# Attention then a gated MLP on one core: MLP work begins with step 21 instead of step 12, and the weights' conversion is spread anew

## The chip, the cores and the metric

The kernel runs on one core of one Trainium2 chip. The metric is the device time of one execution in microseconds (us); a figure for a kernel is the median of several runs. One execution was also taken by the hardware profiler, and all rows of a profile below come from such an execution.

## The reference, cut to what matters

Random-feature attention over 8 batches of 8 heads, 576 rows and 64 columns with 128 features, and a gated MLP on its 4608 output rows (model width 512, inner width 1536). Everything is in 32-bit floats.

```python
def phi(x):
    proj = np.einsum('bhsd,md->bhsm', x, omega)
    sq = np.sum(x * x, axis=-1, keepdims=True) / 2.0
    h = proj - sq
    h = h - np.max(h, axis=-1, keepdims=True)
    return np.exp(h) / np.sqrt(m)
q_p, k_p = (phi(q_s), phi(k_s))
kv = np.einsum('bhsm,bhsd->bhmd', k_p, v)
z = np.sum(k_p, axis=2)
num = np.einsum('bhsm,bhmd->bhsd', q_p, kv)
den = np.einsum('bhsm,bhm->bhs', q_p, z)[..., None] + 1e-06
attn_out = num / den
x = attn_out.transpose(0, 2, 1, 3).reshape(B * S, H * D)
g = x @ w_gate
out = (g * (1.0 / (1.0 + np.exp(-g))) * (x @ w_val)) @ w_out
```

The MLP's three weights arrive as 64-bit floats and are converted by the kernel, word by word, to 32-bit floats.

## The kernel before, in words

**Attention** runs in 72 steps. A step takes two groups of 256 rows of q or k: first twelve groups of k, then a group of q with a group of k in each step. Nine groups make a batch, one of the nine being the odd rest of all heads (its loads are four smaller transfers). The list `ORDER` (L671) sets what a step issues: project x on the features (`st_project`, L377, 16 matrix multiplications in two PSUM banks `pp`), put q's result of three steps ago in transposed form into the MLP's input (`q_out`, L520), transpose the next step's rows (`st_transpose`, L358, bank `pt`; GpSimd squares the rows, L372), multiply q's features with the k-v sums (`q_mult`, L486, bank `po`), accumulate k-v sums (`k_accumulate`, L440), maxima and squares' sums on VectorE (`st_max`, L394), transpose q's features (`q_transpose`, L473, bank `ptq`), and exponentials on ScalarE (`st_exp`, L412, eight of them). The instructions are then put in an order of each engine by the framework; each engine runs its own list in order.

**The MLP** works on ten column tiles of x (256 columns, eight times 512, 256) and on four sets of three inner blocks; one tile with one set is a visit. A visit has 72 multiplications of `mm1` (L550, lines L558; gate `g`, then value `v`) and 9 of `mm2` (L561, L567, output `o`) per 128 rows of the tile. It is written as a generator, `stream` (L600), and yields after every bundle; `give` (L657) draws from it what the plan has due. A product of 32-bit floats is made of three multiplications with high and low parts, which ScalarE (L237, L543, L641) and GpSimd or VectorE (L238, L642, L544) split.

**The conversion** (`convert_all`, L242) takes 36 pieces, three weights for each of twelve inner blocks. A piece has seven ticks: one ScalarE operation (L255), five on VectorE (L257 to L265) and one on GpSimd (L267), of 512 elements in each of 128 partitions; the last also stores the piece to a scratch in memory (L270, on SyncE's queue) and, for the first nine pieces, splits it for the MLP's first set. Every piece loads its raw words first (L220, L225). `need` (L281) forces ticks when the MLP asks for a piece that isn't converted.

**The plan** is made of tables before any instruction is issued. `whole[j]` is the step from which tile j's input is complete (12 for tile 0, 21 for tile 1, 30 for tile 2), `upper` the MLP work that can be done by a step, `lower` what must be, and `course` a smooth line between them: the MLP work to be given by each step. `marks` pairs steps with numbers of pieces that are to be converted by then; in between, ticks follow the plan's clock. `EARLY` (L200) is the step up to which projections of odd steps and the transposed features of q take banks of the MLP's pool (four banks `ps_m`); afterwards projections share two banks and the rest of attention one bank (`ps_a`). `DENSE` (L201) is the same for the transposes of x.

**Queues.** All transfers are issued by SyncE in one list: loads of q, k (`nat`, three buffers, asked for three steps ahead), v, raw weights, stores of converted pieces, loads of weights for later sets, and the output.

Of the kernel before, what the change touches and what calls it, by code (L numbers as in the profile page):

```python
# [23 lines left out]
def kernel(  # L24
# [25 lines left out]
    FA = 3  # L50
# [111 lines left out]
    def visit_us(j):  # L162
        w = TILES[j][1]
        return 2 * FA * mm1_us(w) + w // P * MM2

    cum = np.concatenate([[0.0], np.cumsum([visit_us(j) for j, _, _ in visits])])

    whole, begun = {}, {}
# [5 lines left out]
                begun.setdefault(j, n + OLAG)  # L174


    NN = NS + OLAG + 1
    upper, lower = np.zeros(NN + 1), np.zeros(NN + 1)
    for n in range(NN + 1):
        vi = 0  # L180
        while vi < len(visits) and whole[visits[vi][0]] < n:
            vi += 1
        upper[n] = cum[vi]
        lower[n] = max([0.0] + [cum[last_visit[j - NXB] + 1] for j in begun if j >= NXB and begun[j] <= n])
    lower = np.minimum(lower, upper)
    course = (lower + upper) / 2
    course[0], course[NN] = 0.0, upper[NN]
    for _ in range(20000):
# [3 lines left out]
        course[2:-1:2] = np.clip(mid[1::2], lower[2:-1:2], upper[2:-1:2])  # L192


    clock = course + 4.0 * np.arange(NN + 1)
    marks = [(0, 0.0), (whole[0] - 1, FA), (whole[0] + 2, 3 * FA)]
    for k_ in range(1, NSET):
        at = int(np.searchsorted(course, cum[len(ROUNDS[0]) * k_ - 1]))
        marks.append((max(at, marks[-1][0] + 1), 3 * FA * (k_ + 1)))
    EARLY = whole[0]  # L200
    DENSE = marks[2][0] + 20  # L201

# [130 lines left out]
    def load(n):  # L335
        if n >= NS:
            return
        nats[n] = att.tile([P, 2, CH, 2, D], F32, name=f"nat{n}", tag="nat", bufs=3)
        for kind, src in (("q", q), ("k", k)):
            for i, b, _, gr in slots(n, kind):  # L340
                load_group(nats[n][:, i], src, b, gr, False)
# [16 lines left out]
    def st_transpose(n):  # L358
        if n >= NS:
            return  # L360
        nat = nats.pop(n)
        pt = (ps_moe if n < DENSE else ps_att)(f"pt_{n}", [P, 2, G])
        for i in range(2):
            for c in range(CH):
                nc.tensor.transpose(  # L365
                    pt[:, i, c * P : (c + 1) * P], nat[:, i, c].rearrange("p h d -> p (h d)"), ident
                )
        x = att.tile([P, 2, G], F32, name=f"x_{n}", tag="x")

        st = att.tile([P, 4, 2, CH, 2], F32, name=f"st_{n}", tag="st", bufs=6)  # L370
        sq = att.tile([P, 2, CH, 2, D], F32, name=f"sq_{n}", tag="sq")
        nc.gpsimd.tensor_tensor(sq, nat, nat, op=ALU.mult)  # L372
        nc.scalar.copy(x, pt)
        sts[n] = x, st, sq
        return True

    def st_project(n):  # L377
# [3 lines left out]

        new = ps_moe if n < EARLY and n % 2 else ps_proj
        pp = [new(f"pp{hh}_{n}", [P, 2, CH, M]) for hh in range(2)]
# [89 lines left out]
    def q_transpose(n):  # L473
        m = n
        n -= TLAG
        for _, b, g, gr in slots(n, "q"):
            ph = box.pop(("q", b, g))
            pt = (ps_moe if m < EARLY else ps_att)(f"ptq{b}_{g}", [P, 2, G])
            for hh in range(2):
# [210 lines left out]
    st_transpose(0)  # L690
    for n in range(NN):
        load(n + LA)
# [42 lines left out]
```

## Time and profile before

| | |
|---|---|
| median of three runs | 1291.54 us (1289.42 to 1296.39) |
| profiled execution, its own time | 1285.57 us |
| its span in the profile | 1283.8 us |
| granted TensorE clock, mean | 0.982 |
| idle TensorE in the first 31.6 us | 10.8 us |
| idle TensorE from 31.6 to 217.3 us | 14.0 us |
| idle TensorE from 217.3 us to the end | 15.7 us |

The profile lists the engines' busy time, the chain of work that ended last, groups of equal instructions by line with the mean duration of one, and the busy time of each engine in chosen stretches. TensorE's multiplications are pipelined, so a busy TensorE can still be waiting for its input or running slower than it could. A step is told from the next by the first of its 16 projections (L388): step 4 begins at 31.6 us, step 9 at 50.1, step 12 at 64.0, step 13 at 71.7, step 17 at 121.3, step 20 at 140.0, step 21 at 152.4, step 30 at 217.3 and step 35 at 383.6 us.

### The profile page before, as it was taken

To read this page: it belongs to the slowest core of one execution; us is meant where nothing else is said; L and a number is where in the kernel's file an instruction comes from. 1 tells how busy PE (TensorE), PEld (TensorE's weight loads), DVE (VectorE), ACT (ScalarE), POOL (GpSimd) and SP (SyncE) were. 2 spreads that over 40 slices of the span, in tenths; PEclk is the share of its full clock that TensorE was granted. 3 is DMA by queue.
4 is the path that set the end of the run, shared out by engine and by line. 5 is a ranking of instruction groups with operands and counts; after the bars stand their busy time and mean duration, and the time that the engine had idled before them with its cause. 6 is when DMAs were issued, how large, how long until landed. Compare 5 with 4: busy or idle time off the path is not lost.

```text
span 1283.8 us, 19309 instructions
## 1 busy us (share of the span) xinstructions
PE 1243.3 (97%) x7329; PEld 1039.1 (81%) x7329; DVE 514.2 (40%) x1080; ACT 629.0 (49%) x1358; POOL 419.1 (33%) x364
## 2 busy tenths in 40 slices
PE   6988999999989999999999999999999999999998
PEld 5977778887868888888878888888888878888887
DVE  4787774457742343223333333223333321121212
ACT  4865666565344554555556653854544323222211
POOL 3454241545444121333333311433322113242421
PEclk7997899999989999999999999999999999999999
DMA  6557552345432122221222221211110111111112
GB/s 161 137 159 192 141 160 63 86 136 154 125 95 62 42 67 63 60 64 50 65 59 50 65 51 41 66 50 50 51 41 26 34 33 34 41 43 32 50 27 57
DMA packets 156477, 95.71 MB, mean 75 GB/s; under 512 B 119520, under 2 KB 131808, under 8 KB 156384
## 3 DMA queue, kind: packets, MB, share of 16 engines
q1 hardware_dynamic: 156384, 94.47, 28.0%
q8 instruction: 58, 0.95, 0.3%
q14 instruction: 35, 0.29, 0.1%
HBM read 75.56 MB, written 18.87 MB: 74 GB/s over the span
## 4 chain that ended last, share of the span: by engine, by line
PE 81%; DVE 7%; ACT 3%; issue 3%; POOL 2%; DMA 2%; SPq 1%; POOLq 0%; ACTq 0%; DVEq 0%
PE o L567 21%; PE g L558 21%; PE v L558 19%; PE pp L388 6%; PE kvacc L458 5%; PE po L497 4%; PE ptq L481 2%; PE pt L365 2%; ACT ph L420 1%; PE xt L527 1%; DVE st L261 1%; DVE st L406 1%; POOL wlo L238 1%; DMA nat<-in_k_dram 1%; SPq L323 1%
## 5 line engine op out<-in xcount | busy, mean ns | idle before, releaser
L642 POOL TENSOR_TENSOR hl<-sl,hh 128x512 fp32r<-128x512 f32 (+1 forms) x120 | 145.0, 1208 | 288.9 <-ACT hh L641 285.6
L238 POOL TENSOR_TENSOR wlo<-wraw,whi 128x512 fp32r<-128x512 f32 x108 | 138.9, 1299 | 251.7 <-ACT whi L237 230.0
L420 ACT ACTIVATE ph<-pp,st 128x128 f32<-128x128 f32 x576 | 166.6, 388 | 55.1 <-DVE st L409 54.0
L558 PE MATMUL g<-xh,whi 128*128 128x512 f32 (+1 forms) x480 | 184.4, 387 | 0.5 <-DVE sl L638 0.4
L558 PE MATMUL v<-xh,whi 128*128 128x512 f32 (+1 forms) x480 | 184.0, 383 | 0.0
L567 PE MATMUL o<-whi,hh 128*128 128x512 f32 x432 | 178.1, 412 | 2.4 <-ACT whi L237 1.7
L558 PE MATMUL g<-xl,whi 128*128 128x512 f32 (+1 forms) x480 | 180.0, 375 | 0.0
L558 PE MATMUL g<-xh,wlo 128*128 128x512 f32 (+1 forms) x480 | 178.8, 372 | 0.0
L558 PE MATMUL v<-xh,wlo 128*128 128x512 f32 (+1 forms) x480 | 178.1, 371 | 0.0
L558 PE MATMUL v<-xl,whi 128*128 128x512 f32 (+1 forms) x480 | 177.6, 370 | 0.0
L567 PE MATMUL o<-wlo,hh 128*128 128x512 f32 x432 | 171.5, 397 | 2.0 <-DVE st L408 1.4
L567 PE MATMUL o<-whi,hl 128*128 128x512 f32 x432 | 171.2, 396 | 0.3 <-POOL hl L642 0.2
L641 ACT CAST hh<-sl 128x512 fp32r<-128x512 f32 (+1 forms) x120 | 69.9, 584 | 172.7 <-DVE sl L638 172.3
L638 DVE TENSOR_TENSOR sl<-v,sl 128x512 f32<-128x512 f32 (+1 forms) x120 | 76.3, 636 | 188.0 <-PE v L558 181.9
L372 POOL TENSOR_TENSOR sq<-nat 128x512 f32<-128x512 f32 x72 | 77.4, 1076 | 213.0 <-DMA nat<-in_k_dram 192.8
L591 DVE TENSOR_TENSOR acc<-o,acc 128x512 f32<-128x512 f32 x108 | 74.3, 690 | 178.4 <-PE o L567 177.9
L406 DVE TENSOR_REDUCE st<-pp 128x4 f32<-128x512 f32 x144 | 93.5, 684 | 103.0 <-PE pp L388 103.0
L237 ACT CAST whi<-wraw 128x512 fp32r<-128x512 f32 x108 | 66.9, 623 | 103.9 <-PE v L558 58.5
L558 PEld LDWEIGHTS g<-xh,wlo 128*128 128x128 f32 x480 | 91.3, 190 | 15.2
L558 PEld LDWEIGHTS g<-xh,whi 128*128 128x128 f32 x480 | 91.2, 191 | 15.3 <-DVE sl L638 0.6
L558 PEld LDWEIGHTS v<-xh,wlo 128*128 128x128 f32 x480 | 90.4, 188 | 15.3
L558 PEld LDWEIGHTS g<-xl,whi 128*128 128x128 f32 x480 | 91.6, 191 | 13.2 <-DVE xl L544 0.3
(56 smaller groups left out, 1872.1 us busy)
## 6 DMA issues: line engine op xcount, KB each, us to landing
wraw<-wscr SPq DMA_DIRECT2D x108, 256.0 KB, 2.8
wscr<-wc SPq DMA_DIRECT2D x36, 256.0 KB, 2.2
out_dram<-acc SPq DMA_DIRECT2D x72, 128.0 KB, 2.3
nat<-in_k_dram SPq DMA_DIRECT2D x64, 128.0 KB, 3.1
v<-in_v_dram SPq DMA_DIRECT2D x64, 128.0 KB, 3.1
nat<-in_q_dram SPq DMA_DIRECT2D x64, 128.0 KB, 2.7
st<-in_moe_w_gate_dram SPq DMA_DIRECT2D x12, 512.0 KB, 4.4
st<-in_moe_w_val_dram SPq DMA_DIRECT2D x12, 512.0 KB, 4.6
```

Source lines behind the costliest of these rows:

```text
L237: nc.scalar.copy(hi, raw)
L238: nc.gpsimd.tensor_tensor(lo, raw, hi.bitcast(F32), op=ALU.subtract)
L372: nc.gpsimd.tensor_tensor(sq, nat, nat, op=ALU.mult)
L388: nc.tensor.matmul(pp[hh][:, i, c, :], x[r, i, c * P : (c + 1) * P], omT[r], start=True, stop=True)
L406: nc.vector.tensor_reduce(st[:, 1, :, :, hh], pp[hh], axis=AX.X, op=ALU.max, negate=True)
L420: nc.scalar.activation(ph[:, c, hh * M : (hh + 1) * M], pp[hh][:, i, c, :], AF.Exp, bias=st[:, 3, i, c, hh : hh + 1], scale=1.0,)
L558: nc.tensor.matmul(ps, a_[:, ws], b_[:, c, :], start=n == 0, stop=n == 3 * NC - 1)
L567: nc.tensor.matmul(ps, a_[:, ts_], b_, start=first and n == 0, stop=last and n == 2)
L591: nc.vector.tensor_tensor(a_, po, a_, op=ALU.add)
L638: nc.vector.tensor_tensor(h, pv, h, op=ALU.mult)
L641: nc.scalar.copy(hh, h)
L642: nc.gpsimd.tensor_tensor(hl, h, hh.bitcast(F32), op=ALU.subtract)
```

## The change

`upper` is held at zero through step 21, so the MLP's first visits, of tile 0 and tile 1 with the first set, are planned together in steps 21 to 29. The plan's MLP work per step was 1.4 us in steps 12 to 20 and 2.7 us in steps 21 to 29 (its own units); it is now 0 and 4.1 us. From step 30 on the course is the same. `EARLY` is 21 instead of 12. The marks of the conversion were three pieces by step 11, nine by step 14, and then 18, 27 and 36 by steps 30, 33 and 35; now six by step 21, nine by step 23, and the same three. `DENSE` was 34 and is 35.

```diff
-        upper[n] = cum[vi]
+        upper[n] = cum[vi] if n > whole[1] else 0.0
...
+    EARLY = whole[1]
     clock = course + 4.0 * np.arange(NN + 1)
-    marks = [(0, 0.0), (whole[0] - 1, FA), (whole[0] + 2, 3 * FA)]
+    marks = [(0, 0.0), (EARLY, 2 * FA), (EARLY + 2, 3 * FA)]
     for k_ in range(1, NSET):
         at = int(np.searchsorted(course, cum[len(ROUNDS[0]) * k_ - 1]))
         marks.append((max(at, marks[-1][0] + 1), 3 * FA * (k_ + 1)))
-    EARLY = whole[0]
-    DENSE = marks[2][0] + 20
+    DENSE = marks[-1][0]
```

Lines of the changed kernel are one higher than before from L184 on. In the rows below, `pp0_13` is a projection of step 13, `st_13` its maxima and sums, `v0_1` the MLP's value of visit 0 and block 1, `wc1_1` the piece of block 1 and weight 1 (0 gate, 1 value, 2 output).

TensorE before, in step 13, within the first visit:

```order
L558 MATMUL g0_2_1119<-xh0_657,wlo2_0_533 128x256
L365 MATMUL pt_15_1142<-ident_87,nat15_877 128x128 x4
L458 MATMUL kvacc2_0_1164<-v0_94,ph1_12_980 128x65 x4
L558 MATMUL v0_0_1214<-xh0_657,whi0_1_803 128x256
L558 MATMUL v0_0_1214<-xl0_658,whi0_1_803 128x256
L497 MATMUL po0_5_1047<-kvr0_0_383,qt0_5_969 128x65 x4
L558 MATMUL v0_0_1214<-xh0_657,wlo0_1_804 128x256
```

TensorE of the change, at the same place, step 13:

```order
L389 MATMUL pp1_13_935<-omT_93,x_13_886 128x128
L366 MATMUL pt_14_956<-ident_87,nat14_790 128x128 x4
L482 MATMUL ptq0_6_983<-ident_87,ph0_12_917 128x128 x4
L459 MATMUL kvacc2_0_1050<-v0_94,ph1_12_922 128x65 x2
L528 MATMUL xt0_4_945<-ident_87,xn0_4_899 128x128 x2
L389 MATMUL pp0_14_1008<-omT_93,x_14_961 128x128
```

The MLP's rows are gone from steps 12 to 19; the first of them now stand in step 20 (20 of `g`), and all others of both visits in steps 21 to 29.

VectorE before, behind the last operation of `st_max` of step 12:

```order
L409 SCALAR_TENSOR_TENSOR st_12_821<-st_12_821 128x8
L257 TENSOR_SCALAR wc1_1_847<-wc1_1_847 128x512
L504 TENSOR_SCALAR dn0_4_938<-po0_4_933 128x4
L259 TENSOR_SCALAR wc1_1_847<-wc1_1_847 128x512
L505 RECIPROCAL dn0_4_938<-dn0_4_938 128x4
L261 SCALAR_TENSOR_TENSOR st1_1_801<-st1_1_801,wc1_1_847 128x512
L507 TENSOR_TENSOR xn0_4_941<-po0_4_933,dn0_4_938 128x256
L263 TENSOR_SCALAR wc1_1_847<-st1_1_801 128x512
L257 TENSOR_SCALAR wc2_1_918<-wc2_1_918 128x512
L265 SCALAR_TENSOR_TENSOR wc1_1_847<-st1_1_801,wc1_1_847 128x512
L259 TENSOR_SCALAR wc2_1_918<-wc2_1_918 128x512
L261 SCALAR_TENSOR_TENSOR st2_1_843<-st2_1_843,wc2_1_918 128x512
```

VectorE of the change, behind the same operation:

```order
L410 SCALAR_TENSOR_TENSOR st_12_820<-st_12_820 128x8
L400 TENSOR_REDUCE st_14_962<-sq_14_963 128x8
L264 TENSOR_SCALAR wc1_1_1022<-st1_1_738 128x512
L505 TENSOR_SCALAR dn0_4_896<-po0_4_891 128x4
L266 SCALAR_TENSOR_TENSOR wc1_1_1022<-st1_1_738,wc1_1_1022 128x512
L506 RECIPROCAL dn0_4_896<-dn0_4_896 128x4
L407 TENSOR_REDUCE st_13_887<-pp0_13_934 128x4
L508 TENSOR_TENSOR xn0_4_899<-po0_4_891,dn0_4_896 128x256
L407 TENSOR_REDUCE st_13_887<-pp1_13_935 128x4
```

Ten operations of conversion stood ahead of step 13's maxima; two stand there now. Before, eight pieces are worked on by VectorE in steps 12 to 16 and some five in steps 21 to 29; in the change some three in steps 12 to 20, and twelve in steps 21 to 29.

VectorE of the change, behind the maxima of step 22:

```order
L258 TENSOR_SCALAR wc2_2_1706<-wc2_2_1706 128x512
L545 TENSOR_TENSOR xl2_1314<-xt1_4_1683,xh2_1313 128x256
L260 TENSOR_SCALAR wc2_2_1706<-wc2_2_1706 128x512
L410 SCALAR_TENSOR_TENSOR st_22_1564<-st_22_1564 128x8
L262 SCALAR_TENSOR_TENSOR st2_2_1604<-st2_2_1604,wc2_2_1706 128x512
L505 TENSOR_SCALAR dn1_5_1713<-po1_5_1708 128x4
L264 TENSOR_SCALAR wc2_2_1706<-st2_2_1604 128x512
L506 RECIPROCAL dn1_5_1713<-dn1_5_1713 128x4
L639 TENSOR_TENSOR sl0_2_1666<-v0_2_1758,sl0_2_1666 128x256
```

Between the maxima of steps 22 and 23 ten operations of conversion now stand, where two stood before; some of them, and the MLP's products, stand between the two halves of `st_max`. From step 31 on the lists of VectorE and TensorE have the same instructions in each step as before. ScalarE gets six more loads of its function table (102 in all, 96 before), since its silu and exponentials alternate more often.

## The prediction

> **What bounds the kernel now.** I read the page first, its busy times and the slices.
>
> ```profile
> span 1283.8 us, 19309 instructions
> PE 1243.3 (97%) x7329; PEld 1039.1 (81%) x7329; DVE 514.2 (40%) x1080; ACT 629.0 (49%) x1358; POOL 419.1 (33%) x364
> ...
> PEclk7997899999989999999999999999999999999999
> ...
> PE 81%; DVE 7%; ACT 3%; issue 3%; POOL 2%; DMA 2%; SPq 1%; POOLq 0%; ACTq 0%; DVEq 0%
> ```
>
> TensorE (PE) bounds the kernel as a whole: it is busy for 97% and carries 81% of the chain that ended last. But the early slices have a granted clock below 9 tenths, and the chain has 7% of VectorE (DVE). So I cut the span at the beginnings of the steps in question, taken from the first projection (L388) of steps 12, 21 and 30 in the timeline, and asked for the engines' busy times between them (columns: stretch, its length, busy time of PE, weight loads, DVE, ACT, POOL with instructions, granted clock, DMA share, GB/s).
>
> ```profile
> 64.03 0.49 PE L388 MATMUL pp<-omT,x 64*128 64x128 f32 x4
> ...
> 152.36 0.49 PE L388 MATMUL pp<-omT,x 64*128 64x128 f32 x4
> ...
> 217.29 0.49 PE L388 MATMUL pp<-omT,x 64*128 64x128 f32 x2
> ```
>
> ```profile
> 31.60:50.10 18.50, 18.41 (x189) 16.79 (x188) 14.79 (x36) 15.59 (x51) 7.61 (x7) 1.00 0.65 157
> 50.10:64.00 13.90, 13.55 (x132) 12.44 (x132) 11.04 (x29) 11.76 (x37) 6.19 (x7) 1.00 0.47 111
> 64.00:71.70 7.70, 7.55 (x70) 7.11 (x69) 6.25 (x16) 5.77 (x20) 3.23 (x3) 1.00 0.84 242
> 71.70:121.30 49.60, 40.94 (x269) 34.60 (x268) 42.00 (x81) 27.40 (x69) 28.30 (x23) 0.83 0.61 168
> 121.30:152.40 31.10, 28.51 (x192) 24.72 (x191) 22.83 (x56) 17.70 (x54) 8.74 (x8) 0.89 0.63 162
> 152.40:217.30 64.90, 62.71 (x472) 53.02 (x471) 44.04 (x111) 43.00 (x120) 18.56 (x15) 1.00 0.44 118
> 217.30:383.60 166.30, 158.17 (x872) 132.44 (x871) 94.64 (x161) 85.05 (x156) 76.03 (x60) 0.98 0.39 115
> 383.60:1283.80 900.20, 892.65 (x5019) 739.92 (x5018) 263.83 (x566) 409.66 (x822) 258.49 (x216) 1.00 0.19 49
> ```
>
> The rows are steps 4 to 8, 9 to 11, 12, 13 to 16, 17 to 20, 21 to 29, 30 to 34 and the rest. Steps 9 to 11, the whole of attention without MLP, take 13.9 / 3 = 4.63 us each. Steps 13 to 16 take 49.6 / 4 = 12.4 us each: there VectorE is busy for 42.0 of 49.6 us, TensorE idles for 8.7 us, and its clock is granted at 0.83. That is the one stage which another engine bounds. From 217.3 us on the work is TensorE's again, with 15.7 us of idle time in 1066.
>
> The waits from 64 to 152 us and, for SyncE's queue, from 60 to 217 us show how the stage is tied (columns: who waited for whom, us in total, times, longest):
>
> ```profile
> POOL wc L267 <- DVE wc L265: 24.3, 8, 6.8
> ...
> SPq L270 <- POOL wc L267: 40.3, 15, 4.7
> ```
>
> GpSimd waits for VectorE's conversion, and SyncE's list, behind whose store of a piece (L270) the loads of q and k are queued, waits for GpSimd.
>
> **The MLP work that is moved.** The chain in order of time has runs of multiplications without a gap (start, us, what, count):
>
> ```profile
> 66.98 1.19 PE g L558 x10
> ...
> 582.46 2.82 PE g L558 x12
> ...
> 599.10 2.14 PE o L567 x9
> ```
>
> One of 256 columns takes 1.19 / 10 = 0.119 us, one of 512 takes 2.82 / 12 = 0.235, one of the output 2.14 / 9 = 0.238. The first visit, of 256 columns, is 72 x 0.119 + 18 x 0.238 = 12.9 us. Twenty of its multiplications (2.4 us) now stand in step 20, the other 10.5 us behind step 21. Steps 21 to 29 of before hold 62 of 512 columns and 36 of the output, 14.6 + 8.6 = 23.1 us, so attention costs TensorE (64.9 - 23.1) / 9 = 4.64 us a step beside MLP work, the same as 4.63 without it.
>
> **Steps 12 to 20** took 152.4 - 64.0 = 88.4 us. With the MLP's work and the burst of conversion gone (some three pieces are left on VectorE), they are like steps 9 to 11, which have the same banks, the same loads and a similar rate of conversion: 9 x 4.63 + 2.4 = 44.1 us. The banks matter here: with the old bound of 12 the projections of every step share two banks, and steps 17 to 19, with little MLP work, show what that gives at most:
>
> ```profile
> 121.30:140.00 18.70, 17.84 (x137) 15.75 (x136) 14.63 (x39) 12.93 (x41) 4.55 (x5) 1.00 0.57 143
> ```
>
> That is 6.2 us a step, MLP included; the upper bound is 9 x 6.2 = 56 us. The lower one is the mean of steps 4 to 11, (18.5 + 13.9) / 8 = 4.05, or 38.9 us with the 2.4. I take 44.1, since steps 9 to 11 are the only ones with all of attention and no burst. Hidden here is VectorE, ACT and the transfers: DVE was 11.0 of 13.9 us and ACT 11.8, so neither has much to spare; if one becomes the bound, the bound of 56 us covers it. The loads of q, k and v go with the steps, and the stretch of steps 4 to 8 moved 157 GB/s at 3.7 us a step.
>
> **Steps 21 to 29** get the MLP work and seven pieces. TensorE's need is 9 x 4.64 + 52 x 0.119 + 72 x 0.235 + 54 x 0.238 = 41.8 + 36.0 = 77.8 us, the lower bound. VectorE's need starts from the 44.0 us that it has there now. The first rows are those of 152.4 to 217.3 us, the last two those of 71.7 to 121.3 us (mean ns behind the bar):
>
> ```profile
> L261 DVE SCALAR_TENSOR_TENSOR st<-st,wc 128x512 int32<-128x512 int32 x5 | 4.4, 886 | 0.2
> L265 DVE SCALAR_TENSOR_TENSOR wc<-st,wc 128x512 f32<-128x512 uint32 x5 | 3.5, 690 | 0.0
> L259 DVE TENSOR_SCALAR wc<-wc 128x512 int32<-128x512 int32 x5 | 3.1, 623 | 0.1
> L263 DVE TENSOR_SCALAR wc<-st 128x512 int32<-128x512 int32 x5 | 2.1, 420 | 0.0
> L257 DVE TENSOR_SCALAR wc<-wc 128x512 f32<-128x512 f32 x5 | 2.1, 414 | 0.7 <-ACT wc L255 0.7
> ...
> L261 DVE SCALAR_TENSOR_TENSOR st<-st,wc 128x512 int32<-128x512 int32 x8 | 8.6, 1077 | 0.1
> L263 DVE TENSOR_SCALAR wc<-st 128x512 int32<-128x512 int32 x8 | 5.5, 687 | 0.1
> ```
>
> A piece is 0.886 + 0.690 + 0.623 + 0.420 + 0.414 = 3.03 us of VectorE. Seven more make 21.2; two sums of squares at about 0.68 and three products of 256 columns at about 0.42 (estimates from the sizes of these rows) make 2.7. That is 68 us. Where conversion was dense, L261 took 1.077 and L263 0.687 us, 0.46 us more a piece, so twelve pieces may cost 5.5 us more: 68 to 73.5 us. In steps 13 to 16 the stretch was 49.6 / 42.0 = 1.18 times VectorE's busy time; that factor gives 80 to 87 us, and as VectorE will be about as dense here, this row is nearer than TensorE's bare need. I take 84 us. ScalarE gets some of its six added table loads here, at the duration of the first row below, and 7 x 0.704 us of L255, the second; its 43.0 us grow to about 60 of 84, so it is covered. Should nothing cover the table loads, each stops the exponentials behind it, 6 x 1.3 = 7.7 us, so the upper bound is 87 + 7.7 = 95 us.
>
> ```profile
> L420 ACT ACT_TABLE_LOAD x1 | 1.3, 1283 | 0.0
> ...
> L255 ACT ACTIVATE wc<-st 128x512 f32<-128x512 f32 x8 | 5.6, 704 | 1.3 <-DMA st<-in_moe_w_gate_dram 1.3
> ```
>
> The stores and raw loads of seven pieces also move behind step 21; in SyncE's list they are ahead of loads asked for three steps early, which at 9 us a step have more time than before.
>
> **Sum.** Step 30 began at 217.3 us. It will begin at 64.0 + 44.1 + 84 = 192.1, which is 25.2 us earlier. From there each step has the same work, and TensorE bounds it, so nothing takes the gain back; the one transpose of x that `DENSE` moves to another bank (step 34's) is the same four multiplications, beside MLP work of 26 us a step in the plan. The profiled execution took 1285.57 us (1.8 us lie outside its span) and would take 1260.4; it is 6.0 us below the median of the runs shown, 1291.54, which I use: 1291.5 - 25.2 = **1266 us**. With all lower bounds step 30 begins at 64.0 + 38.9 + 77.8 = 180.7 (36.6 us earlier, 1249 from the profiled execution), with all upper ones at 64.0 + 56 + 95 = 215 (2.3 us earlier, 1289).
>
> Two rules of the Trainium skill bear on this. "Perfetto Trace Analysis", section Optimization Strategy, says that where regimes have different limits, interleaving them may help; this change parts two regimes. By it the stalls of steps 12 to 20 would stay without the MLP to fill them, which is rival 2 below; the rows of steps 4 to 11, 97 to 99% busy without MLP work, don't agree so far. "SBUF — State Buffer", section Who interferes with whom, says that a VectorE instruction with two SBUF inputs is locked out while GpSimd reads. L261 at 886 and 1077 ns agrees, and by the rule twelve pieces beside GpSimd would all pay the higher price, 73.5 us of VectorE and 87 in the sum instead of 84.
>
> **Rivals.** 1. The clock: without MLP work TensorE might be granted half its clock in steps 12 to 20. Step 2 shows the price:
>
> ```profile
> 20.10:27.20 7.10, 7.10 (x39) 6.72 (x38) 4.52 (x8) 4.78 (x16) 5.72 (x5) 0.50 0.77 183
> ```
>
> 7.1 us a step make 9 x 7.1 + 2.4 = 66.3, step 30 at 214.7, so 1291.5 - 2.6 = 1289. For it: clocks of 0.83 and 0.89 where TensorE idled. Against: 1.00 in steps 4 to 11, without MLP work.
>
> 2. The stalls of steps 12 to 20 are attention's own, not the burst's. Then only the moved work goes: 88.4 - 10.5 = 77.9, step 30 at 64.0 + 77.9 + 84 = 225.9, which is 8.6 us later: 1300. Against: VectorE's 42.0 of 49.6 us.
>
> 3. The slower side: in steps 21 to 29 the burst comes back and MLP work doesn't hide beside it, since the conversion, `st_max` and the MLP's products stand in one list of VectorE, while SyncE's loads wait behind the stores. Its price is that of steps 13 to 16, 12.4 us a step, which held 48 x 0.119 + 18 x 0.238 = 10.0 us of MLP, 2.5 a step; now 4.0 a step are due, so 13.9 a step, 125 us, step 30 at 233: 1307. It decides from 217.3 - 64.0 - 44.1 = 109.2 us for the stage, 12.1 us a step. Against: twelve pieces in nine steps are fewer than the eight in five of before, and the first six pieces are converted before the MLP asks for them.
>
> 4. The change does less than it says: VectorE, not spared at 44.1 us, gives steps 12 to 20 at 6.2 us, and steps 21 to 29 at 95: the upper bound, 1289.
>
> **How the numbers follow.** The forecast, with everything between a gain of 7 and 37 us, has 0.82; rival 1 and 4 together 0.08, rival 2 0.05, rival 3 0.05. A measurement of this kernel tells about 0.5% from no change, here 6.5 us: 1285 to 1298. Faster is the forecast, 0.82; rivals 1 and 4 are the same, 0.08; rivals 2 and 3 are slower, 0.10. The range leaves out rivals 2 and 3 and about half of the others: 1249 to 1288 us.
>
> **What would show it.** Right: step 21 begins near 108 us and step 30 near 192; VectorE is over 80% busy in between; the clock is 1.00 in steps 12 to 20; the stretch from step 30 on is 1066 us again. A step 21 later than 120 us at a clock below 0.9 is rival 1, at full clock rival 2; step 30 over 100 us behind step 21 is rival 3. The prediction is wrong if steps 30 to 34 grow, by weights that come late, since then the gain is handed back.

## The result, and the profile after

Before, in the same runs: 1290.48 us (median of four, 1288.29 to 1296.39). After: **1270.01 us** (median of four, 1267.03 to 1272.62). The ratio is 0.9852, 95% interval 0.9822 to 0.9882. The profiled execution of after took 1270.51 us.

The page of after, its span, busy times, granted clock by slices and the chain that ended last by engine:

```profile
span 1268.7 us, 19305 instructions
PE 1235.6 (97%) x7329; PEld 1033.7 (81%) x7329; DVE 509.8 (40%) x1080; ACT 635.7 (50%) x1364; POOL 417.7 (33%) x364
...
PEclk7999999999899999999999999999999999999999
...
PE 78%; DVE 8%; DMA 3%; ACT 3%; issue 3%; POOL 3%; SPq 1%; POOLq 0%; DVEq 0%; ACTq 0%
```

The busy times hardly moved. In the row of the granted clock, slices 4 and 5 (some 95 to 160 us) stood at 7 and 8 tenths before and are now at 9; the first slice and one between 310 and 385 us (the 12th before, the 11th after) are below 9 in both. The stages show where the time went. These are the stretches of after, columns as in the prediction (stretch, length, PE, weight loads, DVE, ACT, POOL, granted clock, DMA share, GB/s); the rows are steps 12 to 20, 21 to 27, 28 and 29, 21 to 29 together, 30 to 34, and the rest:

```profile
65.40:111.50 46.10, 44.02 (x412) 39.27 (x411) 36.74 (x101) 37.08 (x116) 19.20 (x18) 1.00 0.57 142
111.50:174.60 63.10, 61.45 (x447) 52.20 (x446) 51.84 (x118) 48.18 (x115) 27.94 (x23) 1.00 0.56 151
174.60:199.80 25.20, 23.41 (x129) 19.63 (x129) 16.96 (x39) 12.11 (x35) 7.84 (x7) 0.80 0.49 135
111.50:199.80 88.30, 84.86 (x575) 71.83 (x574) 68.80 (x156) 60.29 (x149) 35.78 (x30) 0.94 0.54 146
199.80:368.20 168.40, 160.32 (x883) 134.34 (x882) 97.81 (x167) 88.30 (x160) 79.33 (x63) 0.98 0.43 131
368.20:1268.70 900.50, 892.73 (x5019) 739.94 (x5018) 263.69 (x566) 409.73 (x822) 258.53 (x216) 1.00 0.19 49
```

Steps 12 to 20 fell from 88.4 to 46.1 us, at full clock. Steps 21 to 29 grew from 64.9 to 88.3. From step 30 on it is 1068.9 us against 1066.5 before. The saving of 42.3 us is made in one stage, 23.4 us of it are paid back in the next, and later stages take 2.4 more.

The loss inside steps 21 to 29 sits at their end: 9.0 us a step in 21 to 27, 12.6 in 28 and 29. VectorE's list and then TensorE's there, in order of time (start, us, instruction, in brackets the idle time before it and who ended it):

```profile
178.42 0.43 DVE L258 TENSOR_SCALAR wc<-wc 128x512 f32<-128x512 f32 x1 [2.26 <-ACT wc L256]
...
180.73 1.28 DVE L407 TENSOR_REDUCE st<-pp 128x4 f32<-128x512 f32 x2
...
182.93 0.28 DVE L545 TENSOR_TENSOR xl<-xt,xh 128x128 fp32r<-128x128 f32 x1
```

```profile
184.14 1.56 PE L498 MATMUL po<-kvr,qt 128*128 128x65 f32 x8 [1.79 <-DVE xl L545]
```

VectorE's operation of conversion L258 stood 2.26 us for ScalarE; the step's maxima (L407) and the low parts of the MLP's input (L545) came behind it; TensorE's product of q's features stood 1.79 us for L545, which reads the transposed output in the one bank (`ps_a`) that the product takes next. Then the clock halves. Three stretches of after around it, of 3.4 us each:

```profile
177.80:181.20 3.40, 3.40 (x21) 2.94 (x21) 2.66 (x4) 2.36 (x5) 1.94 (x2) 1.00 0.59 156
181.20:184.60 3.40, 1.61 (x10) 1.06 (x9) 2.88 (x9) 1.36 (x6) 0.58 (x1) 1.00 0.39 125
184.60:188.00 3.40, 3.40 (x14) 2.99 (x14) 2.12 (x6) 2.11 (x6) 1.75 (x2) 0.50 0.63 172
```

TensorE was busy for 1.61 of 3.40 us, and the next 10.2 us ran at half clock.

### The profile page after: what moved, and what is told of

It reads as the page before. It is cut to its first block, busy times and chain, and to the rows that moved or that the text cites. A ratio compares the mean times of both kernels' runs of the same rounds, so it can differ in the third digit from the quotient of the medians.

```text
span 1268.7 us, 19305 instructions
## 1 busy us (share of the span) xinstructions
PE 1235.6 (97%) x7329; PEld 1033.7 (81%) x7329; DVE 509.8 (40%) x1080; ACT 635.7 (50%) x1364; POOL 417.7 (33%) x364
## 4 chain that ended last, share of the span: by engine, by line
PE 78%; DVE 8%; DMA 3%; ACT 3%; issue 3%; POOL 3%; SPq 1%; POOLq 0%; DVEq 0%; ACTq 0%
PE o L568 21%; PE g L559 20%; PE v L559 18%; PE pp L389 5%; PE po L498 4%; PE kvacc L459 4%; PE ptq L482 2%; PE pt L366 2%; DVE st L407 2%; ACT ph L421 1%; DVE st L262 1%; PE xt L528 1%; DMA st<-in_moe_w_gate_dram 1%; DVE wc L258 1%; DMA nat<-in_k_dram 1%
## 5 line engine op out<-in xcount | busy, mean ns | idle before, releaser
L421 ACT ACTIVATE ph<-pp,st 128x128 f32<-128x128 f32 x576 | 168.2, 387 | 53.7 <-DVE st L410 52.8
L568 PE MATMUL o<-whi,hh 128*128 128x512 f32 x432 | 178.1, 412 | 0.9 <-DVE sl L639 0.7
L568 PE MATMUL o<-whi,hl 128*128 128x512 f32 x432 | 171.2, 396 | 0.3 <-POOL hl L643 0.2
L568 PE MATMUL o<-wlo,hh 128*128 128x512 f32 x432 | 170.9, 396 | 0.0
L373 POOL TENSOR_TENSOR sq<-nat 128x512 f32<-128x512 f32 x72 | 76.7, 1066 | 215.8 <-DMA nat<-in_k_dram 190.4
L407 DVE TENSOR_REDUCE st<-pp 128x4 f32<-128x512 f32 x144 | 93.4, 683 | 98.7 <-PE pp L389 98.7
L559 PEld LDWEIGHTS v<-xh,whi 128*128 128x128 f32 x480 | 90.6, 189 | 13.7
```

The costliest lines, as they stand in the source:

```text
L407: nc.vector.tensor_reduce(st[:, 1, :, :, hh], pp[hh], axis=AX.X, op=ALU.max, negate=True)
L421: nc.scalar.activation(ph[:, c, hh * M : (hh + 1) * M], pp[hh][:, i, c, :], AF.Exp, bias=st[:, 3, i, c, hh : hh + 1], scale=1.0,)
L559: nc.tensor.matmul(ps, a_[:, ws], b_[:, c, :], start=n == 0, stop=n == 3 * NC - 1)
L568: nc.tensor.matmul(ps, a_[:, ts_], b_, start=first and n == 0, stop=last and n == 2)
```

## The experiments

The change has three parts: **M**, the MLP is planned from step 21 on; **B**, projections and q's transposed features use the MLP's banks up to step 21 instead of 12; **S**, the conversion is spread instead of a burst in steps 11 to 14. Ratios are to before, on the same chip and in the same runs (before 1288.02 us beside the first four kernels; 1288.46 beside the filler, the 4.9 us stall and the two other shapes; 1288.31 beside the rest).

The order that the framework gives each engine shifts with every edit, so steps 12 to 20 don't hold the same work in every kernel. Counted in the traces, these are the MLP's multiplications on TensorE and the pieces of conversion on VectorE in that stretch:

| | before | B alone | S alone | without B | without S | the change |
|---|---|---|---|---|---|---|
| multiplications | 113 | 99 | 113 | 86 | 45 | 20 |
| pieces | 11 | 10 | 8 | 6 | 8 | 3 |

So the length of that stage is not a bare price of the part that was taken away.

### B alone

```diff
-    EARLY = whole[0]
+    EARLY = whole[1]
```

> The kernel before with one edit: projections of odd steps and q's transposed features use the MLP's banks through step 20. MLP work still begins with step 12, and the burst of conversion still stands in steps 11 to 14. Theory A (the burst of conversion on VectorE makes steps 12 to 20 long): little changes, steps 12 to 20 stay at 78 to 88 us, VectorE over 75% busy in them, 1282 to 1294 us. Theory B (the banks make them long): steps 12 to 20 fall to 55 to 65 us and the time to 1264 to 1274 us. Theory C (MLP work among attention, waiting for its weights, makes them long): unchanged, 1286 to 1294 us.

1276.24 us, 0.9908 [0.9875, 0.994]. Steps 12 to 20 and 21 to 29 of this kernel:

```profile
64.90:135.50 70.60, 62.69 (x494) 55.60 (x493) 61.69 (x141) 51.96 (x140) 34.87 (x29) 0.90 0.64 176
135.50:208.00 72.50, 70.21 (x497) 59.24 (x496) 48.46 (x122) 47.70 (x124) 23.39 (x20) 0.98 0.53 143
```

With the burst and the MLP in place the first stage goes from 88.4 to 70.6 us (14 multiplications of 0.235 us, 3.3 us of it, moved to later steps); TensorE still idles for 7.9 us there and runs at 0.90. The result lies between the two expectations: banks are not a small thing beside the conversion, and not all of it.

### S alone

```diff
-    marks = [(0, 0.0), (whole[0] - 1, FA), (whole[0] + 2, 3 * FA)]
+    marks = [(0, 0.0), (whole[1], 2 * FA), (whole[1] + 2, 3 * FA)]
...
-    DENSE = marks[2][0] + 20
+    DENSE = whole[0] + 22
```

> The kernel before with the marks of the change alone: six pieces by step 21, nine by step 23; MLP work begins with step 12 and forces the pieces that it needs; banks as before. Theory A: steps 12 to 20 hold half as many pieces as before or little more and take 58 to 68 us with their MLP work, 1266 to 1276 us. Theory C: MLP multiplications wait in TensorE's list for pieces that are converted just in time, steps 12 to 20 stay over 76 us, 1282 to 1295 us. Theory B: they stay over 80 us.

1280.89 us, 0.9953 [0.9921, 0.9984]. Steps 12 to 20, then 21 to 29:

```profile
65.20:143.60 78.40, 70.61 (x532) 61.21 (x531) 58.75 (x138) 51.76 (x140) 34.29 (x31) 0.96 0.58 156
143.60:216.70 73.10, 68.78 (x503) 56.59 (x502) 54.14 (x129) 48.14 (x127) 25.27 (x20) 1.00 0.54 152
```

Spreading the conversion takes 10.0 us off the first stage, and 8.2 of them come back in the second, where three of the pieces now stand. The forecast of 58 to 68 us for the first stage failed, because the MLP still forces eight pieces there. The stage stayed over 76 us, as theory C said, but not by its cause: TensorE's waits for converted weights are 1.7 of its 7.8 us of idle time. The time lies between the two forecasts. Step 30 begins only 0.6 us earlier than before; but 18 more of the MLP's multiplications are done by then (113 of them stand in step 30, 131 before), and step 30 takes 25.8 us instead of 31.6.

### The change without B

```diff
-        new = ps_moe if n < EARLY and n % 2 else ps_proj
+        new = ps_moe if n < whole[0] and n % 2 else ps_proj
...
-            pt = (ps_moe if m < EARLY else ps_att)(f"ptq{b}_{g}", [P, 2, G])
+            pt = (ps_moe if m < whole[0] else ps_att)(f"ptq{b}_{g}", [P, 2, G])
```

> The changed kernel with the banks of before: from step 12 on projections share two banks, q's transposed features are in attention's one bank. Late MLP and spread conversion stay. Theory A: steps 12 to 20 take 46 to 54 us, 1268 to 1278 us. Theory B: they take 56 to 65 us or more, 1280 to 1292 us. Theory C: as A.

1293.15 us, 1.0031 [1.0008, 1.0053]: no gain at all, and a little above even theory B. Steps 12 to 20 and 12 to 16 of this kernel, the 3.4 us in which a wait of TensorE for its bank falls (1.36 us for L545), and the 41 us behind them:

```profile
65.20:146.50 81.30, 78.12 (x500) 69.72 (x499) 47.60 (x123) 51.47 (x135) 28.49 (x27) 0.75 0.45 114
65.20:114.40 49.20, 46.72 (x254) 41.44 (x253) 26.49 (x67) 25.25 (x71) 16.04 (x15) 0.58 0.45 109
...
68.20:71.60 3.40, 2.04 (x20) 1.80 (x17) 3.40 (x8) 2.66 (x9) 1.59 (x2) 1.00 0.25 56
71.60:112.60 41.00, 40.03 (x186) 35.48 (x187) 19.45 (x49) 18.25 (x55) 12.18 (x11) 0.50 0.48 117
```

TensorE is busy for 40.0 of 41.0 us, VectorE for less than half, and the clock is 0.50 all the time. No engine keeps TensorE waiting there; it is slow itself. A step takes 9 to 11 us there, and steps 12 to 16 take 49.2 us where the change takes 23.4:

```profile
65.40:88.80 23.40, 21.79 (x201) 19.42 (x200) 19.26 (x50) 19.14 (x59) 10.61 (x10) 1.00 0.47 116
```

This is the prediction's first rival, and the MLP's first 12 multiplications come only at the end of these five steps.

### The change without S

```diff
-    marks = [(0, 0.0), (EARLY, 2 * FA), (EARLY + 2, 3 * FA)]
+    marks = [(0, 0.0), (whole[0] - 1, FA), (whole[0] + 2, 3 * FA)]
```

> The changed kernel with the marks of before: three pieces by step 11, nine by step 14; MLP work still begins with step 21. Theory A: the burst makes steps 11 to 16 long again although no MLP work is there, steps 12 to 20 take 60 to 72 us; steps 21 to 29 have fewer pieces and shrink from 88 to 78 to 82 us; 1276 to 1290 us. Theory C (the burst alone does no harm while no MLP multiplication waits for its pieces): steps 12 to 20 stay below 52 us, steps 21 to 29 shrink, 1258 to 1268 us. Theory B: as C.

1289.84 us, 1.0018 [0.9997, 1.004]. The 3.4 us around the burst's stall (TensorE waits 2.87 us for VectorE, from 79.5 us on), and what follows, behind the row of steps 12 to 20:

```profile
65.80:139.60 73.80, 68.20 (x452) 59.09 (x451) 53.92 (x127) 46.19 (x131) 30.20 (x25) 0.75 0.59 156
...
77.40:80.80 3.40, 2.11 (x16) 1.68 (x16) 3.40 (x5) 1.21 (x2) 2.02 (x2) 1.00 0.50 130
80.80:118.30 37.50, 35.40 (x168) 29.58 (x169) 25.45 (x59) 18.68 (x52) 16.72 (x14) 0.50 0.53 141
```

The stall costs three microseconds; the half clock behind it lasts 37.5 us. The stage took 73.8 us, above the 60 to 72 that my theory gave it, because the theory priced the stall and not the clock behind it. The time is at the upper end of that forecast (1276 to 1290).

The four together, in per cent of before: B -0.9, S -0.5, M with S +0.3, M with B +0.2, all three -1.5. With M, taking either B or S away loses 1.3 to 1.8%. Adding M to S alone costs 12.3 us (1280.89 to 1293.15), adding it to B alone 13.6 us. B with S but without M was not run; if the savings of B and S add up they are 18.9 us, about what all three give (20.5 and 14.7 us in two sets of runs). **Whether M itself gains anything is therefore open.**

### Work instead of waiting: filler for the change without B

As the change without B, with 108 multiplications of 256 columns in steps 11 to 16, written into the MLP's banks and read by nobody.

```diff
...
+            if 11 <= n < 17:
+                fill = ps_moe(f"fill{n}_{i}", [P, T])[:, 0:256]
+                for z in range(2):
+                    nc.tensor.matmul(fill, fw[:, 0:P], fw[:, P : P + 256], start=z == 0, stop=z == 1)
```

> The kernel of e2_nobanks with 108 added multiplications of 256 columns in steps 11 to 16, two after each part of a step, whose products nobody reads (108 x 0.119 = 13 us of TensorE at full clock). They also turn the MLP's four banks, so that transposes of x stand one step ahead. If steps 12 to 16 of e2_nobanks (49.2 us) were long because of the half clock, which lasted 41 us there, the added work ends the spell and these steps take 36 to 42 us although they hold more work: 1278 to 1288 us. If waits for banks made them long and the clock only followed, they take 50 to 62 us and the time is 1294 to 1306 us.

1291.88 us, 1.0035 [1.001, 1.0061]. Steps 12 to 16, and the filler's group on TensorE:

```profile
68.30:106.30 38.00, 35.98 (x314) 32.93 (x312) 26.58 (x66) 23.84 (x71) 14.66 (x13) 1.00 0.56 150
```

```profile
L705 PE MATMUL fill<-fw 128*128 128x256 f32 x108 | 21.7, 310 | 0.0
```

The records show 314 multiplications in the stage instead of 254, 92 of them filler, and it takes 38.0 us instead of 49.2, at clock 1.00. More work took less time, so the slowness was the clock's. The mean clock of the ten executions is 0.983 to 0.990; without filler it is at most 0.974 in eight of ten. But no spell was ended here: none began. TensorE's wait for L545 (L548 in this kernel) is still there, 1.2 us instead of 1.4, so whether the filler works by the work that it adds or by a shorter wait isn't shown. The whole is not faster, against the forecast of 1278 to 1288 us: of the 11.2 us gained, 3.1 are lost ahead of step 12, which begins at 68.3 us instead of 65.2, and 6.3 from step 17 on. The filler also turns over the MLP's banks, so the order of the transposes beside it moves by a step: a confound that this run doesn't remove.

### A stall put in: 4.9 and 2.3 us of VectorE in step 14

The change with one more sum over squares on VectorE behind those of step 14; its result is overwritten. The second form repeats the elements 4 times instead of 9.

```diff
+        if n == 14:
+            nc.vector.tensor_reduce(
+                st[:, 0].rearrange("p i c h -> p (i c h)"),
+                sq.rearrange("p i c h (d o) -> p (i c h) d o", o=1).broadcast_to([P, 8, D, 9]),
...
```

> The changed kernel with one needless VectorE operation in step 14: a sum over nine readings of the same squares, 4608 elements in each partition, about 5 us by the size against 0.68 us for 512. If a stall costs its own length, the time grows by 3 to 6 us, 1272 to 1277 us. If a gap on TensorE among attention's small multiplications sets off a spell of half clock that lasts (41 us in e2_nobanks, 37.5 us in e3_burst, at some 10 us a step instead of 4.6), steps 14 to 20 run at 0.5 for 10 to 40 us and the time grows by 10 to 25 us, 1280 to 1295 us.

1277.78 us, 0.9929 [0.9909, 0.9949], between the two forecasts. The added operation, the 3.5 us around TensorE's gap, and the spell:

```profile
L401 DVE TENSOR_REDUCE st<-sq x1: 4945/4945/4945, 71.4 to 71.4; 128x8 f32<-128x4608 f32 x1
```

```profile
75.70:79.20 3.50, 1.69 (x16) 1.20 (x12) 3.50 (x10) 1.22 (x4) 0.36 (x1) 0.99 0.84 205
79.20:89.40 10.20, 10.14 (x46) 8.80 (x47) 5.14 (x16) 5.19 (x19) 3.01 (x3) 0.50 0.30 73
```

> The change with one added VectorE operation of about 2.2 us in step 14 (a sum over squares whose result is overwritten), where 4.9 us had cost 7.8. Theory, what counts is whether TensorE runs dry for about a microsecond: the projections of the next step stand ahead, so 2.2 us leave a gap of under 1 us or none, no half clock, and the kernel is 0 to 3 us slower than the change. Rival, any stall of VectorE in these steps sets off half clock: a spell of 7 to 10 us shortly behind step 14 and 5 to 10 us more in all.

1274.34 us, 0.989 [0.9874, 0.9906], against 1273.63 for the change itself in the same runs. The added operation took 2.28 us. TensorE's longest gap in the steps behind it, 1.6 us, begins at 86.5 us, 12 us later, in step 16. The granted clock can change at 83.8, 87.2 and 90.6 us in this trace (the steps of 3.41 us of the last section), and the gap lies across the second of these times:

```profile
83.80:87.20 3.40, 2.65 (x30) 2.23 (x28) 3.22 (x8) 1.82 (x4) 2.54 (x3) 1.00 0.51 117
87.20:90.60 3.40, 2.57 (x24) 2.60 (x25) 3.40 (x10) 2.92 (x10) 1.25 (x1) 1.00 0.15 34
```

The 4.9 us left TensorE idle for 1.8 of 3.5 us, and 10.2 us of half clock followed. The gap of 1.6 us was split, 0.7 us in one stretch and 0.9 in the next, and the clock stayed at 1.00. So a gap of over a microsecond isn't enough by itself, as my theory had it: it matters how much of it falls into one stretch. The theory's cost (0 to 3 us) was met with 0.7 us between the medians; its gap (under 1 us) was not, and since the gap comes so late, that the added operation made it isn't shown. Steps 12 to 20 took 45.9 us in the change beside it, 49.3 with the 2.3 us at full clock, and 52.8 with the 4.9 us; one more piece of conversion stands in them in both kernels. The two operations differ in length as well as in what the clock did, so they don't give the price of the half clock alone.

### Two other shapes: an even conversion, and banks lent up to step 30

```diff
-    marks = [(0, 0.0), (EARLY, 2 * FA), (EARLY + 2, 3 * FA)]
+    marks = [(0, 0.0), (EARLY, 3 * FA)]
```

> The changed kernel with nine pieces converted by step 21 and then evenly to 18 by step 30, so that steps 21 to 29 have ten pieces on VectorE instead of twelve and steps 12 to 20 five instead of three. If VectorE sets the length of steps 21 to 29 (88.3 us for 68.8 us of VectorE in the changed kernel), they shrink by 2 x 3.1 x 1.2 = 7 us, and steps 12 to 20, which TensorE sets, stay at 46 to 50 us: 1263 to 1270 us. If single stalls and spells of half clock set it, there is no proportion: steps 21 to 29 between 82 and 95 us, 1265 to 1278 us.

1276.58 us, 0.9928 [0.9905, 0.995]. Steps 21 to 29 take 78.8 us with ten pieces instead of twelve, and steps 12 to 20 take 53.9 with the two others (and with 21 multiplications of the MLP that stand behind step 21 in the change):

```profile
72.20:126.10 53.90, 50.18 (x442) 43.94 (x441) 44.70 (x115) 42.21 (x125) 24.35 (x21) 0.97 0.57 150
126.10:204.90 78.80, 73.33 (x536) 62.02 (x535) 61.36 (x141) 56.07 (x139) 27.87 (x24) 1.00 0.55 153
```

The two stages together, 132.7 us, are no longer than in the change (134.4 and 132.8). What makes this kernel slower lies ahead of them: a fifth piece is converted before step 12, TensorE's gap of 1.5 us at 55.9 us is followed by 6.8 us of half clock, and step 12 begins at 72.2 us instead of 65.4. So steps 21 to 29 shrank about as the first theory said (by 7 us), while the time came out in the second theory's range for a reason that neither had.

For the second one, `EARLY` in the two bank choices (the lines of the change without B) is replaced by `whole[2]`, step 30.

> The changed kernel with the MLP's banks lent to projections of odd steps and to q's transposed features through step 29 instead of step 20. Transposes of x then stand at most one step ahead in TensorE's list through step 30. If banks (and the order that they give) are what keeps steps short, steps 21 to 29 shrink from 88.3 us towards TensorE's need of 78: 1260 to 1267 us. If VectorE sets that stage, it stays at 86 to 92 us, 1268 to 1274 us; if MLP work now waits for banks, it grows over 92 us.

1274.51 us, 0.9905 [0.9872, 0.9938]. Steps 12 to 20 are the best of all runs, 21 to 29 the worst:

```profile
65.60:108.50 42.90, 40.38 (x381) 35.81 (x380) 35.25 (x94) 34.48 (x107) 17.30 (x16) 1.00 0.54 139
108.50:206.80 98.30, 89.79 (x607) 77.23 (x606) 69.95 (x165) 62.85 (x158) 36.90 (x31) 0.90 0.52 141
```

Steps 12 to 20 are shorter than the change's mainly because 20 of the MLP's multiplications (2.4 us) moved out of step 20. In steps 21 to 29 TensorE idles for 8.5 us and its clock drops to 0.90, but little of that is a wait for the MLP's banks: 6.5 us are q's product (L498) waiting for VectorE's L545, which holds attention's one bank, and 1.8 us are L568 waiting for ScalarE to empty an output. The time of this stage met the third forecast (over 92 us), its cause didn't. Lending up to step 21 pays (the change against the change without B), and lending longer gains nothing more.

### The rest of the loss: steps 28 and 29, and the start

The change again, on the chip of the three below:

> The changed kernel again, beside the next three on one chip. Theory (a gap of TensorE of over a microsecond among attention's small multiplications sets off some microseconds of half clock, and the change leaves steps 12 to 20 without such a gap): step 21 at 110 to 114 us, no half clock between steps 12 and 20, and the loss of steps 28 and 29 (a gap of 1.8 us and 10 us of half clock) again within 2 us of its place if it belongs to the order of the lists, elsewhere or gone if it is chance; ratio to before 0.983 to 0.988.

1273.63 us, 0.989 [0.9873, 0.9908]: 14.7 us faster than before, a little less than expected; the two intervals of the change overlap. Steps 12 to 20 and 21 to 29:

```profile
65.80:111.70 45.90, 43.95 (x411) 39.26 (x410) 37.42 (x101) 37.05 (x116) 18.87 (x18) 1.00 0.56 143
111.70:198.60 86.90, 83.22 (x575) 70.59 (x574) 68.75 (x156) 60.27 (x149) 36.19 (x30) 0.96 0.54 148
```

TensorE's gap of 1.8 us came at 182.7 us, where it was in the first trace (182.3), with half clock behind it again. It belongs to the order of the lists. Over all fourteen traces 13 spells of half clock begin in steps 21 to 29, and for 11 of them this wait of L498 for L545 is TensorE's longest gap in the 3.4 us before (worked out from the traces' records). TensorE's list needs attention's one bank again before VectorE, whose list the conversion fills, has read it.

With a fourth buffer for raw words:

```diff
-            u = moe.tile([P, DM], F32, name=f"wc{f}_{i}", tag="wraw", bufs=3)
+            u = moe.tile([P, DM], F32, name=f"wc{f}_{i}", tag="wraw", bufs=4)
...
-        raw = moe.tile([P, DM], F32, name=f"wraw{f}_{i}", tag="wraw", bufs=3)
+        raw = moe.tile([P, DM], F32, name=f"wraw{f}_{i}", tag="wraw", bufs=4)
```

> The change with four buffers instead of three for raw words and their conversion, so that VectorE's next piece has been touched by ScalarE earlier. Theory, the stall of steps 28 and 29 comes from the conversion's chain over engines (VectorE stood 2.26 us for ScalarE's operation of the same piece): the stall and its 10 us of half clock go, steps 21 to 29 take 81 to 85 us instead of 88.3, the kernel 1263 to 1268 us. Rival, the stall is of VectorE's density there and any order of its list meets it: 87 to 92 us for the stage, 1268 to 1274 in all.

1277.86 us, 0.9916 [0.9901, 0.9932]. Steps 21 to 29 take 86.9 us as in the run beside it, and the wait is still there, at the same operation:

```profile
178.80 0.95 DVE L258 TENSOR_SCALAR wc<-wc 128x512 f32<-128x512 f32 x1 [1.72 <-ACT wc L256]
```

My theory falls in its form: the buffer isn't what delays ScalarE's operation there. What does was not found. A new gap of 5.1 us in step 31, with 6.8 us of half clock behind it, made this kernel slower.

With the conversion begun at step 3 and two raw loads ahead of the steps:

```diff
-    marks = [(0, 0.0), (EARLY, 2 * FA), (EARLY + 2, 3 * FA)]
+    marks = [(0, 0.0), (3, 0.0), (EARLY, 2 * FA), (EARLY + 2, 3 * FA)]
...
-        load_raw(0)
...
-            load_raw(n + 1)
+            if n:
+                load_raw(n + 1)
...
+    load_raw(0)
+    load_raw(1)
```

> The change, with the first two raw pieces loaded ahead of the steps and the conversion's ticks begun at step 3 instead of step 0. Theory, a gap starts the spell: if the conversion's first pieces are what lets TensorE idle for 3.6 us at 14.8 us, the gap goes and with it much of the 17.1 us of half clock in steps 1 to 3; those steps take 14 to 18 us instead of 23.1 and the kernel 1261 to 1267 us. Rival, the spell at the start is the clock's own beginning or the gap is the loads' of q and k: steps 1 to 3 stay at 22 to 25 us and the kernel at 1268 to 1274.

1271.71 us, 0.9885 [0.9853, 0.9917], no different from the change, as the rival said. TensorE's gap of 4 us in step 1 didn't go, so the edit didn't test what it was made for. But the profiled execution was the longest of six (1283.04; the others 1267.11 to 1275.96), and its trace shows a long spell of half clock. The rows are step 5, step 6, step 7, step 8, and the half clock in them as one stretch:

```profile
32.20:42.80 10.60, 9.28 (x64) 8.71 (x62) 4.35 (x10) 7.52 (x28) 3.90 (x4) 0.70 0.52 126
42.80:46.30 3.50, 3.50 (x25) 3.16 (x24) 1.41 (x3) 0.41 (x1) 1.04 (x1) 0.50 0.48 114
46.30:55.60 9.30, 9.30 (x51) 8.61 (x50) 2.85 (x8) 4.66 (x16) 1.04 (x1) 0.50 0.49 125
55.60:62.70 7.10, 7.10 (x43) 6.76 (x42) 3.63 (x11) 3.31 (x10) 1.04 (x1) 0.50 0.31 75
...
36.50:67.20 30.70, 30.70 (x171) 28.76 (x169) 12.61 (x30) 14.29 (x44) 4.80 (x5) 0.50 0.44 113
```

A gap of 1.3 us at 33.1 us was followed by 30.7 us of half clock, in steps 5 to 9, which the trace of before shows at 1.00.

## Why the prediction came out right, step by step

**Step 12 at 64.0:** 65.4. The start has a half-clock spell of 13.7 us in the trace of before and 17.1 in that of after; TensorE's list up to step 12 is the same in both kernels.

**Steps 12 to 20 at 44.1 us:** 46.1. The size held, and that the banks matter held too. The reason was too narrow. I took the stage for VectorE's burst and the MLP, with the banks as a smaller matter, at most 56 us. The runs show that with M both others are needed: M with the burst gives 73.8 us (without S), M with shared banks 81.3 (without B, far above my bound), and with all three it is 46.1. That M is needed too isn't shown.

**Steps 21 to 29 at 84 us:** 88.3, the term that was mis-sized. VectorE's need was right, 68.8 against 68. These are the five operations of a piece in steps 21 to 29 of after:

```profile
L266 DVE SCALAR_TENSOR_TENSOR wc<-st,wc 128x512 f32<-128x512 uint32 x12 | 9.5, 793 | 0.2
L262 DVE SCALAR_TENSOR_TENSOR st<-st,wc 128x512 int32<-128x512 int32 x12 | 8.7, 729 | 0.3
L260 DVE TENSOR_SCALAR wc<-wc 128x512 int32<-128x512 int32 x12 | 7.4, 614 | 0.1
L264 DVE TENSOR_SCALAR wc<-st 128x512 int32<-128x512 int32 x12 | 6.4, 533 | 0.1
...
L258 DVE TENSOR_SCALAR wc<-wc 128x512 f32<-128x512 f32 x12 | 5.4, 452 | 3.1 <-ACT wc L256 2.9
```

A piece is 3.12 us (3.03 in the prediction). The higher price that I drew for all twelve pieces from the Trainium skill's "SBUF — State Buffer", Who interferes with whom, didn't come: L262 took 0.729 us on average, not 1.077. The records of its twelve operations show why: nine had no GpSimd instruction beside them and took 0.68 to 0.70 us, and of the other three one took 1.19. In the whole trace of after, 24 of 36 ran with GpSimd beside them for under a tenth of their time, at 0.69 us on average, and 10 with it beside them for over half, at 1.30. So the rule agrees with the trace; that each piece would meet GpSimd was my assumption. What failed is the factor 1.18 on VectorE's time. It is no property of the stage: it is 1.28 here (88.3 / 68.8), 1.28 with ten pieces (78.8 / 61.4) and 1.41 with the banks lent longer (98.3 / 70.0). Seen from TensorE, the stage is its need of 77.8 us, 3.4 us of idle time, and a half-clock spell of 10.2 us, which costs some 5 us if the same work takes half as long at full clock (an estimate): 86.3 of the 88.3 us, and the rest is open. Seven steps without such a spell took 9.0 us each, which would be 81 for nine.

**Step 30 at 192.1, 25.2 us earlier:** 199.8, 17.5 earlier, by the differences above (1.4 + 2.0 + 4.3 = 7.7).

**From step 30 on unchanged at 1066 us:** 1068.9. Thirteen MLP multiplications more (144 instead of 131) fall into step 30, 13 x 0.235 = 3.1 us. I had not counted any carried over. I had named growing steps 30 to 34 as a sign of being wrong, by weights that come late; they grew, from 166.3 to 168.4 us, but TensorE's idle time in them is 8.1 us in both, so it is work and not a wait. VectorE was busy for 78% of steps 21 to 29, just under the 80% that I had named as a sign of being right.

**The sum:** 1266 forecast, 1270.0 and 1273.6 measured in two sets of runs; all inside the range. The gain is 15 to 20 us where 25.2 were forecast, and the stage that gives it came out near its size for more reasons than I had, which is in part luck.

**Rival 1, the clock,** is the one that I priced too low and dismissed on weak evidence. It didn't happen in the change, but the traces of both kernels that have M without B or without S show it, at some 10 us a step instead of my 7.1 (and its sum is 214.3, not 214.7, which changes nothing). "1.00 in steps 4 to 11" was no evidence against it: the last experiment shows steps 5 to 9 at 0.50.

**Rival 2, attention's own stalls:** partly so. S takes 10.0 us and B 17.8 us off the stage with the MLP in place (3.3 of the 17.8 are moved work), so the burst is one cause and the shared banks another. The rule beside it, that regimes with different limits be interleaved (the Trainium skill, "Perfetto Trace Analysis", Optimization Strategy), is borne out where the banks are shared: there the kernel with the MLP among attention (S alone, 1280.89) beats the parted one (1293.15), and with filler the clock stayed up. The change does without interleaving there: with B and S, TensorE's longest gap in that stage is 0.7 us.

**Rival 3, the burst back in steps 21 to 29,** needed 109.2 us; the stage took 88.3, and 98.3 in its worst form. **Rival 4** didn't occur: VectorE's spare time of 9.4 us in 46.1 was enough.

How much of the gain is clock? The mean granted clock of an execution is 0.978 for before (median of 60 executions), 0.9875 and 0.9845 for the two sets of the change, 0.9735 without B, 0.974 without S, 0.988 with filler. Among 56 executions of before between 1280.98 and 1291.56 us, 0.001 of clock goes with 0.92 us (correlation -0.94). By that, 6 to 9 of the 15 to 20 us gained are clock, and the rest would be waits that went away. This is an estimate from a spread, not a separate measurement.

## What to carry to other kernels

Before moving the work of a busy engine out of a stage, ask where its gaps will fall and what follows them when that work is gone: here 1.4 to 2.9 us of waiting were followed by up to 41 us at half clock. Parts of a schedule change can each be harmless or useful alone and lose in pairs, so run them apart and in pairs, and run the pair that leaves out the headline part. Price a stage by the bounding engine's own need plus its gaps and the half clock behind them, not by a factor from another stage.

## What the runs showed of the hardware

**Half a short window idle is enough for half clock.** The granted clock changes in steps of 3.41 us. I cut the first 400 us of the fourteen traces into these windows and summed TensorE's idle time in each (worked out from the traces' records):

```
window at full clock, TensorE idle    windows   next window at half clock
under 0.9 us                             1328      0
0.9 to 1.6 us                              36      8
1.6 us and more                            46     45
```

The Trainium skill, "TensorE: Matmul & The Clock Gate", Part 1, gives a free-running window of 3413 ns and a return to half clock after an idle window. The window agrees, and so does that it runs free: a gap of 1.8 us that fell into one window of the change's trace was followed by half clock, and one of 1.6 us that was split over two (the 2.3 us operation) was not. That also fits the differences between executions of one kernel (1267 to 1283 us in the last experiment). That the window must be idle does not agree; from about 1.6 of 3.41 us on it was enough.

**Full work doesn't always end it.** Of 172 windows at half clock, 53 were the last of their spell, all with under 0.6 us of idle time; but 72 others had under 0.1 us of it and the spell went on. The spells of 30 to 41 us all lie among attention's small multiplications without MLP work (but for the last 1.5 us of the longest), though the profile calls TensorE busy throughout; those beside MLP work ended after at most 14 us, but some without it, too, after 7 to 10, and those of the first steps after 13.7 to 17.1. That it is the density of the small multiplications which keeps the clock down is my reading; no run tests it, since no spell began beside the filler.
